# A transformer block on one core: when w2's first split is made, which banks attention takes, and a last product in full precision

## The chip, the core and the metric

The kernel runs on one core of a Trainium2 chip. The core has five engines with queues of their own: TensorE (PE, matrix products and transposes), VectorE (DVE), ScalarE (ACT), GpSimd (POOL) and SyncE (SP), which here only issues transfers. Each engine takes its instructions in program order, and an instruction that waits holds back all that stands behind it on the same engine. The metric is the device time of one execution in microseconds (us).

## What is computed

The reference adds to its input an attention over 16 heads and an MLP. Sizes: 2048 tokens of 448, 16 heads of 28 that share one key and one value, a hidden width of 1792, all in float32.

```python
xn = _layernorm(x)                                   # 2048 x 448
q = (xn @ wq).reshape(B, S, 16, 28).transpose(0, 2, 1, 3)
k, v = xn @ wk, xn @ wv                              # one head of 28
p = softmax(einsum("bhqd,bkd->bhqk", q, k) * 28 ** -0.5)
att = einsum("bhqk,bkd->bhqd", p, v) ... @ wo
mlp = gelu(_layernorm(xn) @ w1 + b1) @ w2 + b2       # gelu in its tanh form
out = x + att + mlp
```

The MLP normalises once more what is normalised already; the kernel folds both into one scale and shift per token (`lnq`, `lnqb`, beside `lnr`, `lnb` for the first alone).

## The kernel before

**Tiles.** The tokens lie in 16 tiles of 128. Four tiles make a chunk (`c`, 512 tokens, the width of a PSUM bank in float32). The core's eight PSUM banks are handed out by pools: `mp` has three, the others change from stage to stage. `mtile` takes the next bank of a ring of pools.

**Precision.** Most products run in the faster fp32r type with a value split into a high share and a low share: `wah`/`wal`, `w1h`/`w1l`, `w2h`/`w2l`, `hh`/`hl`, `oth`/`otl`, `woh`/`wol`, `xh`/`xl`. A split is one ACT copy (which rounds to the high share) and one subtraction on DVE or POOL. A product then takes three matmuls: high by high, high by low, low by high. Products of probabilities and values run in full float32, where the trace records each matmul twice.

**Stages.**

1. The front, about 0 to 66 us: for each chunk the statistics of the norm (`bn` L214 for one tile, `bn_end` from L216 for a chunk, with `rstd` L199 to L205), the centred rows (`center` L290 on ACT and L291 on POOL for columns 384 to 448), their transposes (`turn` L299 on PE, L300 on ACT, L301 on DVE) and four query slots (`q_slot`: PE L181 to L186, and an `evac` one slot later with DVE L390, ACT L391, DVE L398). Queries go to the DRAM tiles `qd` through the SBUF tiles `qe`, issued on the SP queue by L405. The first query slot also gives keys and values. Between the slots lie the splits of w1 (`w1_split`: ACT L355, POOL L356 and L357), in eight parts. Where each stands is written out by hand: in the tuple at L505, and in the table `more` filled at L438 to L459. The last argument of `later`, `ahead`, puts a job ahead of the slot's centring and turning.

2. The MLP, 66 to 463 us: 56 slots, one for each chunk and each of 14 blocks of 128 hidden columns. Slot n does `mlp1` of its own block (11 matmuls into one PSUM bank, `ph`; ACT L652 and L653 empty it; then POOL L654 and L655, ACT L658, POOL L659 and L660, ACT L665 for `hh`, POOL L667 for `hl`) and `mlp2` of the block of slot n - 2 (12 matmuls at L684, into four banks). The parts of the chain behind `mlp1` hang between the matmuls of `mlp2` by a table called `stages`. `ph` has one bank; slot 1 uses one of the four `m2` banks, which are not needed by then. w2's splits (`w2_split`: ACT L369, then `low`, L373 on DVE and on POOL, which also issues the next load of w2) stand in the slots of the first chunk. Between all those matmuls two further streams run: the row maxima for attention (`max_stream`: PE L570, DVE L571) and the turned scores (PE L604, DVE L605, ACT L622, stored to `td` by L625). Their pace is counted at L753 to L767.

3. Attention, 463 to 1068 us: 16 units of a chunk and four heads. Each step makes scores (PE L953), exponentials (ACT L954) and bursts of products of probabilities with values (PE L925) into a bank of the pool `op`. Seven banks in a ring serve the scores and the maxima. The row sums come out of the same products, and `norm_jobs` divides by them.

4. The end, for the last unit alone: `pv_halves` (L899) makes the last products in two halves of 256 tokens, one half in the `op` bank and one in the bank of `mp1`, which leaves the ring at that point. `end_jobs` (L865) divides each half by its row sums (DVE L879 to L882), splits it (ACT L883, DVE L884), multiplies with `woh` and `wol` (PE L815 to L817) and adds the sum to the rows (`rows`, from DRAM tile `ad`) by L819. The results leave by L821, on the ACT queue for odd tiles and on the SP queue for even ones. Matmuls of the identity (`spin`, L427) are put between the halves.

**What sets the order.** The program is emitted under a manual schedule, so on each engine the instructions run in the order in which Python emits them. Waits between engines follow from the tiles: who writes, who reads, and whose memory a tile takes over. The memory of `w2h` and `w2l` (pool `hp`, opened at L634) was before that of tiles of the front that were closed at L523.

Of the kernel before, what the change touches and what calls it, by code (L numbers as in the profile page):

```python
# [16 lines left out]
P = 128  # L17
S, D, H, DH, F = 2048, 448, 16, 28, 1792
NT = S // P
CT = 4  # L20
# [20 lines left out]
def block_kernel(ctx, tc, x, wq, wk, wv, wo, w1, b1, w2, b2, out):  # L41
# [322 lines left out]
    def w2_split(s):  # L364
        raw = wl_q.pop(0)
        ab = slice(2 * s, 2 * s + 2)

        def high():
            act.activation(w2h[:, ab, :], raw, AF.Copy)  # L369

        def low():
            for eng, b in ((dve, 0), (pool, 1)):
                eng.tensor_sub(w2l[:, 2 * s + b, :], raw[:, b], f(w2h[:, 2 * s + b, :]))  # L373
            if s + 2 < NF // 2:
                w2_load(s + 2)

        return high, low
# [103 lines left out]
    for c in range(NCH):  # L481
        if c + 1 < NCH:
            center, turn = norm_parts(c + 1, False, bank=lambda shape: (qbank, mtile)[next(turns) % 2](shape))
        for i in range(4):
# [20 lines left out]
            if i in ((2, 3), (1, 3), (1, 3), (0, 2))[c]:  # L505
                n = 2 * c + (i // 2 if c == 3 else i // 3)
                w1_split(n)
                if n < 2:
                    w1_load(n + 4)
                elif n == 3:  # L510
                    w1_load2(6)
                elif n in (4, 5):
                    w2_load(n - 4)
                if n == 2:
                    qms.append(load_m(*heads[0], q=pool))
                elif n in (4, 5):
                    load_m(TURNED[n - 4], 3, q3[n - 4], pool)
# [176 lines left out]
    def slot(n):  # L694
        nonlocal maxed, ending, later_low
# [30 lines left out]
    norms, maxed, ending, later_low = {}, 0, none, none  # L726
# [7 lines left out]
    for n in range(len(mslots) + 2):  # L734
# [73 lines left out]
    def o_jobs(c, gs, tiles=range(CT)):  # L808
        last = NG - 1 in gs
        for k in tiles:  # L810
# [9 lines left out]
            if last:  # L820
                (nc.scalar if k % 2 and c == NCH - 1 else nc.sync).dma_start(ov[:, CT * c + k, :], a)  # L821
# [43 lines left out]
    def end_jobs(u, pos, weighted):  # L865
# [3 lines left out]
        oth, otl = o_tiles(c, g)  # L869
        jobs = o_jobs(c, [g])  # L870
        tr, rb, on = att.tile([P, CW], F32, name="tr2", bufs=1), att.tile([P, CW], F32, name="tr", bufs=1), att.tile([P, CW], F32, name="oc", bufs=1)
# [5 lines left out]
        def shares(i):  # L877
# [4 lines left out]
            dve.tensor_mul(on[:, h], pos[i], rb[:, h])  # L882
            act.activation(oth[:, h], on[:, h], AF.Copy)  # L883
            return lambda: dve.tensor_sub(otl[:, h], on[:, h], f(oth[:, h]))  # L884
# [14 lines left out]
    def pv_halves(u, kt):  # L899
        nonlocal ring  # L900
# [135 lines left out]
```

## Time and profile before

| What | us |
|---|---|
| median of three runs | 1078.68 |
| those runs, lowest and highest | 1078.29, 1080.1 |
| the profiled execution's own time | 1079.98 |
| its span on the core | 1078.2 |

The granted TensorE clock of the profiled execution is 0.999. The span is what the profiler saw between the first and the last instruction on the core; the execution's own time has about 1.8 us more around it.

The profile's lines are read so. A line of the timeline has the start and the length in us, the engine, the line of the kernel, the operation, output <- input with the program's names, shape and type, and the number of instructions that follow each other; square brackets hold the idle time of the engine before it and what ended it. `PE` is a matmul, `SPq` or `ACTq` an instruction of an engine's queue that issues a transfer or handles a semaphore. A line of the windows has a stretch of the span, the busy time of PE, its weight loads, DVE, ACT and POOL with the number of instructions started, and then the granted clock, the mean busy share of the DMA engines and GB/s. A line of the waits has the engine and line, what it waited for, and total, times and longest. A group has the busy time, the mean in ns of one, and the idle time before them.

### The profile page before, as it was taken

The numbers are of one execution on the slowest core, as the hardware profiler recorded it, in microseconds if no ns is written. First come the engines' busy times: TensorE is split into PE (matmuls) and PEld (weight loads), VectorE is DVE, ScalarE is ACT, GpSimd is POOL, SyncE is SP. The second block draws the span as 40 slices with busy tenths as digits, with TensorE's granted clock in tenths as the row PEclk, the third lists the DMA queues.
The fourth block names the chain that finished last, engine by engine and source line by source line (L and its number), as shares of the span: only waits on it lengthen the run. The fifth ranks groups of instructions, "written<-read, shape, count | busy, mean of one in ns | idle before, by whom it ended". The sixth has DMA issues, their size and how long they took to land.

```text
span 1078.2 us, 17653 instructions
## 1 busy us (share of the span) xinstructions
PE 1068.5 (99%) x5869; PEld 720.0 (67%) x5869; DVE 906.7 (84%) x1825; ACT 721.8 (67%) x1254; POOL 574.8 (53%) x722
## 2 busy tenths in 40 slices
PE   9999999999999999999999999999999999999998
PEld 8778888888888888855555556555556555555455
DVE  6889999988988998977998997899896999876744
ACT  5675556666667666569677775677774777865784
POOL 5678897678777888744333532433352243243220
PEclk9999999999999999999999999999999999999999
DMA  8775546677877778687887798678896778985820
GB/s 268 242 214 150 143 126 175 167 190 189 211 179 195 181 209 220 157 181 165 184 200 186 173 218 193 160 188 195 194 205 174 180 168 189 213 191 141 187 43 35
DMA packets 139367, 193.54 MB, mean 179 GB/s; under 512 B 17078, under 2 KB 95084, under 8 KB 139276
## 3 DMA queue, kind: packets, MB, share of 16 engines
q1 hardware_dynamic: 126028, 169.59, 62.8%
q0 software_dynamic: 11840, 22.25, 9.1%
q8 instruction: 46, 0.75, 0.3%
q10 hardware_dynamic: 1408, 0.57, 0.2%
q14 instruction: 45, 0.37, 0.1%
HBM read 113.38 MB, written 77.71 MB: 177 GB/s over the span
## 4 chain that ended last, share of the span: by engine, by line
PE 96%; DVE 2%; ACT 1%; POOL 1%; issue 0%; POOLq 0%; ACTq 0%; DVEq 0%
PE po L925 21%; PE m L570 19%; PE m L953 17%; PE m L684 12%; PE ph L181 10%; PE m L604 5%; PE qp L181 2%; PE m L815 1%; PE m L816 1%; PE m L817 1%; PE ph L186 1%; PE ph L184 1%; PE m L427 1%; PE po L908 1%; PE m L908 1%
## 5 line engine op out<-in xcount | busy, mean ns | idle before, releaser
L571 DVE TENSOR_REDUCE mx<-m 128x1 f32<-128x512 f32 x784 | 507.3, 679 | 76.1 <-PE m L570 66.0
L954 ACT ACTIVATE p<-m 128x512 f32<-128x512 f32 x784 | 402.6, 609 | 160.8 <-PE m L953 160.6
L570 PE MATMUL m<-ks,qm 128*128 128x512 f32 x784 | 321.1, 410 | 0.7 <-DVE half L786 0.5
L953 PE MATMUL m<-xh,ks 128*128 128x512 f32 x784 | 257.4, 397 | 0.0
L925 PE MATMUL po<-p,vs 128*32 128x512 f32 x1920 | 230.9, 598 | 0.0
L570 PEld LDWEIGHTS m<-ks,qm 128*128 128x128 f32 x784 | 147.0, 187 | 114.9 <-ACT p L954 41.3
L605 DVE TENSOR_SCALAR_CACHE_REDUCE raw<-m 128x512 f32<-128x512 f32 x240 | 162.5, 690 | 17.5 <-PE m L604 10.6
L953 PEld LDWEIGHTS m<-xh,ks 128*128 128x128 f32 x784 | 146.1, 188 | 42.4 <-issue 6.2
L936 DVE STREAM_TRANSPOSE p<-half 128x1024 f32<-128x1024 f32 x120 | 148.3, 1236 | 5.3 <-PE m L908 2.0
L622 ACT ACTIVATE raw<-raw,m 128x1024 f32<-128x1024 f32 x120 | 133.1, 1150 | 0.8 <-DVE m L611 0.8
L925 PEld LDWEIGHTS po<-p,vs 128*32 128x32 f32 x1920 | 50.1, 109 | 114.0 <-issue 109.0
L652 ACT ACTIVATE hx<-ph,b1t 128x512 f32<-128x512 f32 x55 | 37.9, 690 | 129.9 <-PE ph L186 109.2
L604 PE MATMUL m<-ks,q 128*128 128x512 f32 x240 | 94.1, 392 | 0.1
L667 POOL TENSOR_TENSOR hl<-hx,hh 128x512 fp32r<-128x512 f32 x56 | 72.6, 1296 | 29.8 <-ACT hh L665 29.8
L684 PE MATMUL m<-w2l,hh 128*128 128x448 f32 x224 | 80.7, 365 | 1.3 <-DVE w2l L373 1.3
L684 PE MATMUL m<-w2h,hh 128*128 128x448 f32 x224 | 81.0, 364 | 0.0
L684 PE MATMUL m<-w2h,hl 128*128 128x448 f32 x224 | 80.8, 366 | 0.1
L557 POOL DMA_DIRECT2D xh<-mn x15 | 8.1, 539 | 133.5 <-ACT mn L553 133.5
L472 POOL DMA_DIRECT2D qm<-qd x120 | 61.6, 521 | 28.7 <-PE m L953 22.6
L655 POOL TENSOR_TENSOR hz<-hz,hx 128x512 f32<-128x512 f32 x56 | 72.7, 1298 | 4.7
L660 POOL TENSOR_TENSOR hx<-hx,hz 128x512 f32<-128x512 f32 x56 | 72.5, 1294 | 4.7
L535 POOL DMA_DIRECT2D xh<-qd x60 | 38.0, 634 | 51.4 <-PE m L570 49.1
(183 smaller groups left out, 1411.9 us busy)
## 6 DMA issues: line engine op xcount, KB each, us to landing
td<-raw SPq DMA_DIRECT2D x240, 256.0 KB
half<-td SPq DMA_DIRECT2D x120, 512.0 KB
xh<-qd POOLq DMA_DIRECT2D x60, 168.0 KB, 4.2
qm<-qd POOLq DMA_DIRECT2D x120, 56.0 KB, 4.3
qd<-qe SPq DMA_DIRECT2D x24, 256.0 KB
a<-in_A_x_dram SPq DMA_DIRECT2D x24, 224.0 KB
qm<-qd SPq DMA_DIRECT2D x76, 56.0 KB
ad<-a SPq DMA_DIRECT2D x16, 224.0 KB
```

The costliest lines, as they stand in the source:

```text
L181: pe.matmul(ps, w, v, start=(n == 0), stop=False)
L570: pe.matmul(pm, qm[:, t * P:(t + 1) * P], ks[:, n * CW:(n + 1) * CW], start=True, stop=True)
L571: dve.tensor_reduce(mx[:, CT * j + t, n:n + 1], pm, axis=AX.X, op=ALU.max)
L604: pe.matmul(sc, q3[i][:, t * P:(t + 1) * P], ks[:, n * CW:(n + 1) * CW], start=True, stop=True)
L605: dve.tensor_scalar(raw[:, :, 4 * n:4 * n + 4, :].rearrange("p r b i -> p b r i"), sc.rearrange("p (b r i) -> p b r i", r=4, i=32), SCALE, ...
L622: act.activation(raw[:, rs], raw[:, rs], AF.Exp, bias=m3[:, 4:5], scale=1.0)
L655: pool.tensor_mul(hz, hz, hx)
L684: pe.matmul(m2[k], h[:, k * P:(k + 1) * P], w[:, ft, :], start=(ft == 0 and i == 0), stop=(ft == NF - 1 and i == 2))
L925: pe.matmul(po[32 * j:32 * j + 32, :], vs[:, kt, :], ps.pop((u, kt, j)), start=(kt == 0), stop=(kt == NT - 1))
L936: dve.transpose(p.rearrange("p k (g j) -> p g k j", j=32), halves[u, kt // 8][:, :, 32 * (kt % 8):32 * (kt % 8) + 64].rearrange("p g (k j) ...
L953: pe.matmul(s, ks[:, kt * P:(kt + 1) * P], qss[u][:, j, :], start=True, stop=True)
L954: act.activation(p, s, AF.Exp, scale=SCALE)
```

## The change

It has five parts.

- Statistics of the front: three `bn` of chunk 2 stand at slot (0, 1) and one at (0, 2); those of chunk 3 stand at (1, 0), (1, 1), (1, 2) and (1, 3), the first of them not ahead of the slot's turning but behind it. Before, they stood one position later.
- w1's first split stands at slot (0, 1) in place of (0, 2); the load of w1's fifth part stays at (0, 2).
- w2's first split (`w2_split(0)`) is emitted whole at the start of slot 0, with both low halves on POOL. Before, its high half came in the stages of slot 0 and its low half in slot 2 behind `mlp1`, one half on DVE and one on POOL. The load of w2's third part, which `low` issues, moves with it.
- The last two slots of the MLP take their two row maxima early, and attention opens its pools in another order: `op` before `mp1`, and `mp1` fourth in the ring. At the end `mp1` leaves the ring seven steps before the last.
- In `end_jobs` the last product runs in full float32 on the divided values with `wor`; the splits, the spins and the twelve fp32r matmuls go. The row tile of k = 1 is added by a matmul with the identity and copied out by ACT; the other three are added by DVE.

```diff
@@ w2_split
         def low():
-            for eng, b in ((dve, 0), (pool, 1)):
+            for eng, b in ((pool if s == 0 else dve, 0), (pool, 1)):
                 eng.tensor_sub(w2l[:, 2 * s + b, :], raw[:, b], f(w2h[:, 2 * s + b, :]))
@@ front
-    for c, at in ((2, ((0, 1), (0, 2), (0, 2), (0, 3))), (3, ((1, 1), (1, 2), (1, 3), (2, 0)))):
+    for c, at in ((2, ((0, 1), (0, 1), (0, 1), (0, 2))), (3, ((1, 0), (1, 1), (1, 2), (1, 3)))):
         for k in range(CT):
-            later(*at[k], lambda t=CT * c + k: bn(t), c == 3)
+            later(*at[k], lambda t=CT * c + k: bn(t), c == 3 and k > 0)
...
-            if i in ((2, 3), (1, 3), (1, 3), (0, 2))[c]:
+            if (c, i) == (0, 2):
+                w1_load(4)
+            if i in ((1, 3), (1, 3), (1, 3), (0, 2))[c]:
                 n = 2 * c + (i // 2 if c == 3 else i // 3)
                 w1_split(n)
-                if n < 2:
-                    w1_load(n + 4)
+                if n == 1:
+                    w1_load(5)
@@ slot
             if n == 0:
-                high, later_low = w2_split(0)
+                for job in w2_split(0):
+                    job()
...
-        if n == 2:
-            later_low()
...
         if n == 0:
-            stages = {0: texp, 1: middle, 2: high}
+            stages = {0: texp, 1: middle}
@@ the loop over the slots
         if n >= len(mslots):
-            done, pace = 0, (2, 6)[ft]
+            done = 0
...
-            if n >= len(mslots) and done % pace == 1:
+            if n >= len(mslots) and (done % 2 if ft == 0 else done <= 2):
                 maxed += mxs.step()
@@ attention
     mp3 = ctx.enter_context(tc.tile_pool(name="mp3", bufs=3, space=PSUM))
+    op = ctx.enter_context(tc.tile_pool(name="op", bufs=1, space=PSUM))
     mp1 = ctx.enter_context(tc.tile_pool(name="mp1", bufs=1, space=PSUM))
-    op = ctx.enter_context(tc.tile_pool(name="op", bufs=1, space=PSUM))
-    ring = itertools.cycle([mp] * 3 + [mp3] * 3 + [mp1])
+    ring = itertools.cycle([mp] * 3 + [mp1] + [mp3] * 3)
@@ end_jobs
             dve.transpose(blocks(rb, h), rc[:, r, None].to_broadcast([P, 8, 32]))
-            dve.tensor_mul(on[:, h], pos[i], rb[:, h])
-            act.activation(oth[:, h], on[:, h], AF.Copy)
-            return lambda: dve.tensor_sub(otl[:, h], on[:, h], f(oth[:, h]))
+            for k in (0, P):
+                at = slice(256 * i + k, 256 * i + k + P)
+                dve.tensor_mul(on[:, at], pos[i][:, k:k + P], rb[:, at])
+
+        sums = {}
+
+        def product(k):
+            first = k not in sums
+            if first:
+                sums[k] = mtile([P, D])
+            pe.matmul(sums[k], on[:, k * P:(k + 1) * P], wor[:, g, :], start=first, stop=True)
+
+        def result(k):
+            a = rows[c, k]
+            if k == 1:
+                act.activation(a, sums[k], AF.Copy)
+            else:
+                dve.tensor_add(a, a, sums[k])
+            (nc.scalar if k % 2 else nc.sync).dma_start(ov[:, CT * c + k, :], a)
 
         weighted(0)
-        low = shares(0)
-        low()
+        shares(0)
         weighted(1)
-        spin(9, mtile([P, P]))
-        low = shares(1)
-        next(jobs)
-        low()
-        for _ in jobs:
-            pass
+        sums[1] = mtile([P, D])
+        pe.matmul(sums[1], ident, rows[c, 1], start=True, stop=False)
+        product(0)
+        product(1)
+        shares(1)
+        for k in (2, 3):
+            product(k)
+        for k in range(CT):
+            result(k)
@@ pv_halves and the loop over the steps
             pos[u] = [op.tile([P, CW], F32, name="po")[:, 0:256], mp1.tile([P, CW], F32, name="m")[:, 0:256]]
-            ring = itertools.cycle([b for b in (next(ring) for _ in range(7)) if b is not mp1])
...
+        if n == len(steps) - 7:
+            ring = itertools.cycle([b for b in (next(ring) for _ in range(7)) if b is not mp1])
```

More of the change, by code (lines that the diff above doesn't have):

```diff
@@ L694, in slot @@
     def slot(n):
-        nonlocal maxed, ending, later_low
+        nonlocal maxed, ending
         middle = high = low = none
@@ L724, in none @@
         pass
-    norms, maxed, ending, later_low = {}, 0, none, none
+    norms, maxed, ending = {}, 0, none
     mslots = [(c, ft) for c in range(NCH) for ft in range(NF)]
@@ L820, in o_jobs @@
             if last:
-                (nc.scalar if k % 2 and c == NCH - 1 else nc.sync).dma_start(ov[:, CT * c + k, :], a)
+                nc.sync.dma_start(ov[:, CT * c + k, :], a)
             yield
@@ L868, in end_jobs @@
         c, g = units[u]
-        oth, otl = o_tiles(c, g)
-        jobs = o_jobs(c, [g])
-        tr, rb, on = att.tile([P, CW], F32, name="tr2", bufs=1), att.tile([P, CW], F32, name="tr", bufs=1), att.tile([P, CW], F32, name="oc", bufs=1)
+        tr, rb, on = (att.tile([P, CW], F32, name=n, bufs=1) for n in ("tr2", "tr", "oc"))
         rc = att.tile([P, CW // 32], F32, name="rc", bufs=1)
@@ L881, in shares @@
             dve.transpose(blocks(rb, h), rc[:, r, None].to_broadcast([P, 8, 32]))
-            dve.tensor_mul(on[:, h], pos[i], rb[:, h])
-            act.activation(oth[:, h], on[:, h], AF.Copy)
-            return lambda: dve.tensor_sub(otl[:, h], on[:, h], f(oth[:, h]))
+            for k in (0, P):
[14 more added lines that the diff above has]
+            (nc.scalar if k % 2 else nc.sync).dma_start(ov[:, CT * c + k, :], a)
         weighted(0)
-        low = shares(0)
-        low()
+        shares(0)
         weighted(1)
-        spin(9, mtile([P, P]))
-        low = shares(1)
-        next(jobs)
-        low()
-        for _ in jobs:
-            pass
+        sums[1] = mtile([P, D])
[7 more added lines that the diff above has]
+            result(k)
     pos, ps, pairs = {}, {}, {}
     def pv_halves(u, kt):
-        nonlocal ring
         if kt == 0:
             pos[u] = [op.tile([P, CW], F32, name="po")[:, 0:256], mp1.tile([P, CW], F32, name="m")[:, 0:256]]
-            ring = itertools.cycle([b for b in (next(ring) for _ in range(7)) if b is not mp1])
         def weighted(i, kts):
```

## The prediction

> **What bounds the kernel now.** I read the page's busy shares first, then the chain of work that ended last, then TensorE's waits.
>
> ```profile
> PE 1068.5 (99%) x5869; PEld 720.0 (67%) x5869; DVE 906.7 (84%) x1825; ACT 721.8 (67%) x1254; POOL 574.8 (53%) x722
> PE 96%; DVE 2%; ACT 1%; POOL 1%; issue 0%; POOLq 0%; ACTq 0%; DVEq 0%
> ...
> PE m L684 <- DVE w2l L373: 1.3, 1, 1.3
> ...
> PE m L570 <- DVE half L786: 0.5, 1, 0.5
> PE m L815 <- ACT oth L883: 0.5, 1, 0.5
> ```
>
> TensorE is busy for 99% of the span and carries 96% of the last-ending chain. Its few waits happen once each, and the three quoted (waited in total, times, longest) are the ones that this diff touches. Only a wait removed or added, or TensorE work removed or added, moves the end: no PE gap behind a shift absorbs it, so a shift early in the span reaches the end at its full size. That makes the rest a matter of four places: front, start of the MLP, MLP to attention, and end.
>
> **Start of the MLP (w2's first split).** Before, the split's ACT half (L369) comes after slot 0's L652, L653 and L658, and its low halves (L373, one on DVE, one on POOL) only in slot 2. Afterwards L369 stands on ACT directly behind the last L391, ahead of L652 of slot 0, and both L373 stand on POOL ahead of L654. The wait that goes is the 1.29 us below. What the move exposes is the memory under w2h: it is that of the front's qe buffers, so L369 may write it only after the last of the front's stores from qe to qd (L405) has landed.
>
> ```profile
> 65.92 1.20 ACT L391 ACTIVATE qe<-qp 128x512 fp32r<-128x512 f32 x2 [0.57 <-ACT w1h L355]
> 68.47 0.69 ACT L652 ACTIVATE hx<-ph,b1t 128x512 f32<-128x512 f32 x1 [1.35 <-PE ph L186]
> 69.05 0.68 ACT L653 ACTIVATE hz<-ph,b1s 128x512 f32<-128x512 f32 x1
> 71.94 0.63 ACT L658 ACTIVATE hz<-hz 128x512 f32<-128x512 f32 x1 [0.27 <-POOL hz L655]
> 72.47 0.94 ACT L369 ACTIVATE w2h<-raw 128x896 fp32r<-128x896 f32 x1
> 74.69 0.63 ACT L665 ACTIVATE hh<-hx 128x512 fp32r<-128x512 f32 x1
> ...
> 64.61 4.70 SPq L405 DMA_DIRECT2D qd<-qe  x8
> ...
> 71.50:72.00 0.50, 0.50 (x4) 0.42 (x3) 0.50 (x2) 0.23 (x2) 0.41 (x1) 1.00 0.01 4
> 72.00:72.25 0.25, 0.25 (x3) 0.21 (x2) 0.25 (x1) 0.25 (x1) 0.00 (x0) 1.00 0.00 0
> ...
> L369 ACTq EVENT_SEMAPHORE  x4: 38/38/161, 71.9 to 72.3; - x4
> ...
> 69.89 0.63 POOL L654 TENSOR_SCALAR hz<-hz 128x512 f32<-128x512 f32 x1 [2.07 <-ACT hz L653]
> 76.62 1.28 POOL L667 TENSOR_TENSOR hl<-hx,hh 128x512 fp32r<-128x512 f32 x1
> ...
> L373 POOL TENSOR_TENSOR w2l<-raw,w2h 128x448 fp32r<-128x448 f32 x7 | 8.1, 1162 | 0.0
> ...
> 72.30 0.39 PE L181 MATMUL ph<-xh,w1h 128*128 128x512 f32 x1
> 75.70 0.36 PE L684 MATMUL m<-w2h,hh 128*128 128x448 f32 x1
> 78.43 0.66 PE L684 MATMUL m<-w2l,hh 128*128 128x448 f32 x2 [1.29 <-DVE w2l L373]
> 79.79 0.77 PE L684 MATMUL m<-w2h,hl 128*128 128x448 f32 x3
> 80.84 0.39 PE L181 MATMUL ph<-xh,w1h 128*128 128x512 f32 x1
> ```
>
> The SP queue issues the eight stores back to back until 64.61 + 4.70 = 69.31 us. The DMA share (second column from the end) falls to 0.01 only in 71.5 to 72.0 and to nothing in 72.0 to 72.25. ACT's sequencer still spent 161 ns, against 38 for the others, on one of the four waits put in front of L369, between 71.9 and 72.3. So the stores land at about 72.2, and before, L369 at 72.47 simply came late enough. Ahead of L652 it has no such cover: ACT is free at 65.92 + 1.20 = 67.12 and would stand until 72.5. Queued behind it on ACT are L652 and L653 of slot 0 (who empty the one ph bank), then that slot's turned exponentials and L658; on POOL L654 and L655.
>
> Step by step:
> - L369 runs 72.50 to 73.35 (next start 0.85 later, as 72.47 to L652 in the old order), L652 to 73.93, L653 to 74.61. TensorE's next use of ph, slot 2's mlp1, starts at 74.66 in place of 72.30: **+2.36**. Its block lasts 75.70 - 72.30 = 3.40 and ends at 78.06.
> - POOL makes both low halves from 73.5 (2 x 1.16 and a little between: 75.88), then L654. From L654's start to L665's end took 74.69 + 0.63 - 69.89 = 5.43 before, all of it one chain (L654, L655, L658, L659, L660, L665), so hh is there at 81.31. The first product with w2h starts at 81.35 instead of 75.70: **+5.65**, with a second gap of 81.35 - 78.06 = 3.3 us.
> - From there the products do not wait for w2l: 80.84 - 75.70 = 5.14 less 1.45 (the 1.29 and what the restart adds at its edges) gives 3.69, to 85.04. hl comes from L660's end (80.6), L654 and L655 for slot 1 (0.63, and about 1.3 as for L667, a tile of the same size) and L667 (1.28): 83.9; the products that need it are due at 81.35 + (79.79 - 75.70 - 1.45) = 83.99. In time.
> - The next mlp1 needs ph emptied by ACT, whose L652 waits for L667 to give hx back (83.9), then 0.58 + 0.68: 85.2. Against 80.84 this is **+4.3** net, the 1.45 gain included.
>
> Bounds: the stores could have landed at 72.0, which gives 3.9; at 72.3 and with 0.1 more at each of the handovers 4.6. The added SP step, the load of the next w2 pair, waits in its queue for L373 and has only the first td stores behind it, which only attention reads.
>
> **Front.** w1's first split (ACT 0.94, POOL's two) moves ahead of an L391 at 20 us; three bn_stats of chunk 2 move together into (0,1); chunk 3's start one position earlier, one of them before L390 instead of after it.
>
> ```profile
> 28.73 1.02 DVE L199 TENSOR_SCALAR rs<-lnp 128x4 f32<-128x4 f32 x2
> 42.25 0.62 DVE L214 BATCH_NORM_STATS2 st<-hl 128x6 f32<-128x448 f32 x1
> 43.18 0.55 DVE L199 TENSOR_SCALAR rs<-lnp 128x4 f32<-128x4 f32 x2
> ...
> 28.01 1.64 POOL L356 TENSOR_TENSOR w1l<-raw,w1h 128x672 fp32r<-128x672 f32 x1
> 42.00 1.63 POOL L356 TENSOR_TENSOR w1l<-pair,w1h 128x672 fp32r<-128x672 f32 x1 [0.76 <-ACT w1h L355]
> ```
>
> Taking the bn at 42.25 out looks like a gain, but L199 does not end by its own length: the first pair ends at 29.75, 0.10 after POOL's L356 ends (29.65), the second at 43.73, 0.10 after 43.63. So at 43 us nothing comes earlier, as long as POOL's L356 stays where it is. At 28 us L356 itself comes some tenths earlier, since the first split no longer stands ahead of it on POOL and ACT, but the chunk-3 bn ahead of L390 (0.62) takes that back before TensorE sees it. I take **0.0**. Low end -1.2, if L199 got in ahead of L356 at both places and a bn of 0.62 were saved at each; high end +0.6, one bn on the path. The Trainium skill, "GPSIMD Engine Reference", 1. Specifications, has GpSimd's SBUF access shared with VectorE, with contention for some DVE instructions. By that rule L199 stays held and the front gives 0; without it the front would give up to 1.2, and the two equal ends above bear the rule out.
>
> **MLP to attention.** The last slot's row maxima are spread differently: the second of them now falls into the wait for hl. Attention's PSUM ring takes op before mp1 and hands out mp1 fourth, so the fourth bank no longer waits for L689's last add; the fifth does.
>
> ```profile
> 461.42 0.68 PE L684 MATMUL m<-w2h,hl 128*128 128x448 f32 x2
> 463.40 0.40 PE L953 MATMUL m<-xh,ks 128*128 128x512 f32 x1
> 463.61 1.14 DVE L689 TENSOR_TENSOR a<-a,m 128x448 f32<-128x448 f32 x2
> 464.80 0.50 PE L570 MATMUL m<-ks,qm 128*128 128x512 f32 x1 [0.54 <-DVE half L786]
> ...
> 465.57 3.05 ACT L954 ACTIVATE p<-m 128x512 f32<-128x512 f32 x6 [0.59 <-PE m L953]
> ```
>
> The products with hl wait a moment for L667 ahead of 461.42; a maximum fills that. Matmuls of 512 columns start 0.23 apart (15 of them in the 3.40 from 72.30 to 75.70), so the first score comes 0.23 earlier. Then the fourth matmul no longer waits to 464.80; the next one waits for L689's end, 464.75 less about 0.4 (0.23 from the products, the rest because no maximum stands between the adds any more): 464.35. ACT's third exponential follows at 464.8 instead of 465.57. ACT paces the next steps, so I take **-0.75**; bounds -0.3 (the shift at the first score alone, with the bank wait back one matmul later) and -1.0. Once the ring turns, it is the same seven banks.
>
> **End.** Nine spins and twelve fp32r products (woh, wol, otl) give way to one identity product that adds the row tile, and four products in full fp32; L883 and L884 go.
>
> ```profile
> 1070.01 0.42 DVE L884 TENSOR_TENSOR otl<-oc,oth 128x256 fp32r<-128x256 f32 x1 [0.48 <-ACT oth L883]
> 1070.35 0.44 DVE L879 STREAM_TRANSPOSE tr<-m 128x256 f32<-128x256 f32 x1
> 1071.54 0.42 DVE L882 TENSOR_TENSOR oc<-m,tr 128x256 f32<-128x256 f32 x1
> 1072.79 1.88 DVE L819 TENSOR_TENSOR a<-a,m 128x448 f32<-128x448 f32 x3
> ...
> 1068.48 2.27 PE L427 MATMUL m<-ident 128*128 128x128 f32 x18
> ```
>
> No fp32 product of 448 columns is in the trace. The spins are fp32, each on record twice: 18 records of 128 columns in 2.27, the last of which shows its whole pipeline; at some 0.111 a record, 448/128 = 3.5 and two records give 0.78. From below, an L684 product's 0.20 spacing (fp32r, same columns) times three is 0.6; from above 2.27/18 x 3.5 x 2 = 0.88. I take 0.78.
> The second transpose no longer has the L884 and its 0.48 wait in front, only the second half of a multiply: it starts at about 1069.52, 0.83 earlier, so the second half's first multiply starts near 1070.75 and the block's third product at 1071.1 (the identity product and the first two products lie before it, from 1068.5 to 1070.95). Two products of 0.78 end at 1072.66, 0.17 more to be seen: DVE's last add runs 1072.87 to 1073.48. Before, the last of the three ended at 1072.79 + 1.88 = 1074.67. The stores behind stay the same: **-1.2**; by the bounds of the product -0.8 to -1.5.
>
> **The sum.** +4.3 + 0.0 - 0.75 - 1.2 = +2.35. The profiled execution took 1079.98 us (1078.2 of span and 1.8 around it); with the change 1082.3. It lay 1.30 above the median 1078.68, so beside the runs shown the forecast is 1081.0. Its own range is 1079.9 (3.9 - 0.2 - 1.0 - 1.5 = 1.2) to 1082.2 (4.6 + 0.3 - 0.5 - 0.9 = 3.5).
>
> **Rivals.**
> B, the clock drops in the second PE gap. For it: TensorE starts slow, as these rows of the spins show:
>
> ```profile
> 4.00:8.00 4.00, 4.00 (x23) 4.00 (x22) 3.17 (x13) 2.60 (x5) 2.25 (x4) 1.00 1.04 329
> 8.00:12.00 4.00, 4.00 (x38) 4.00 (x37) 3.08 (x15) 2.67 (x6) 2.31 (x7) 1.00 0.94 267
> ```
>
> 23 matmuls in 4 us, then 38. A gap of 3.3 us with one of 2.4 before it could bring that back. Against it: after the 1.29 us wait at 78.43 the products keep their 0.2. No row has a longer gap. At half speed for some 4 to 5 us, about half of that is lost: +2.2, 1083.2. The Trainium skill, "TensorE: Matmul & The Clock Gate", Part 1, puts the return to the slow clock after about 3.4 us without work and its practical table warns of gaps over some 3 us; by that rule the gap here is at the edge, and the time would be 1083.2.
> C, the front's chain runs free: 1081.0 - 1.2 = 1079.8. Against it the two ends at POOL's L356 above.
> D, the other side: L369 doesn't wait, because the stores have landed before slot 0's ph is full (by about 68.5). Then the stall goes (-1.45), with -0.75 and -1.2 it makes -3.4: 1075.3. It decides at ACT's L369: a start before 68.5. Against it stands the DMA share until 71.5; for it, that the 161 ns may be another semaphore's.
> E, the end gains nothing, since fp32 products take two to four times the estimate or the reordered tail waits elsewhere: 1081.0 + 1.2 to 1.9, some 1082.6.
>
> **Chances.** Forecast 0.56, B 0.20, C 0.06, D 0.12, E 0.06. Two in ten are left out by 1078.2 to 1084.2, which takes in C, B and E and leaves out D with some over. 0.2% is 2.16 us (about what a measurement tells from no change), so slower begins at 1080.84 and faster at 1076.5: slower holds B, E and a little over half of the forecast (0.32), 0.58; faster is D, 0.12; within 0.30.
>
> **What would show it.** ACT's L369 waiting from 67.1 to about 72.5, a PE gap near 70 to 74.7 and one near 78 to 81.3, no gap at the first w2l product, and the slot-3 mlp1 4.3 later; L199 still ending with POOL's L356; the third L954 of attention 0.75 earlier relative to the slots before it; products in full fp32 about 0.78 apart. If L369 starts before 70 the forecast is wrong at its main term; if the matmuls between 81 and 86 are spaced twice as far, B holds.

## The result and the profile after

| | median us | runs | lowest to highest |
|---|---|---|---|
| before | 1078.99 | 8 | 1078.26 to 1080.12 |
| changed | 1082.39 | 8 | 1081.65 to 1083.66 |

The ratio is 1.0032, with a 95% interval of 1.0021 to 1.0043: the change costs 2.3 to 4.6 us, 3.4 by the medians. The profiled execution took 1081.89 us, with a span of 1080.0.

The first view is TensorE's waits of the changed kernel (total, times, longest). Line numbers have moved: from L508 to L700 they are two higher than before, further down by another amount (L786 is L787, L908 is L923, L953 is L968).

```profile
PE m L686 <- ACT hh L667: 2.9, 1, 2.9
PE ph L181 <- ACT hz L655: 1.5, 1, 1.5
...
PE m L968 <- DVE half L787: 0.2, 1, 0.2
```

The wait for w2l is gone, and two waits that weren't there head the list. Next, the timelines of SP, ACT, POOL and TensorE at the start of the MLP:

```profile
62.52 5.42 SPq L405 DMA_DIRECT2D qd<-qe  x8
...
65.18 1.20 ACT L391 ACTIVATE qe<-qp 128x512 fp32r<-128x512 f32 x2 [0.57 <-ACT w1h L355]
70.99 0.95 ACT L369 ACTIVATE w2h<-raw 128x896 fp32r<-128x896 f32 x1 [4.62 <-DVE mx L573]
71.85 0.67 ACT L654 ACTIVATE hx<-ph,b1t 128x512 f32<-128x512 f32 x1
72.42 0.68 ACT L655 ACTIVATE hz<-ph,b1s 128x512 f32<-128x512 f32 x1
...
79.10 0.63 ACT L667 ACTIVATE hh<-hx 128x512 fp32r<-128x512 f32 x1 [0.93 <-POOL hx L662]
...
72.02 2.24 POOL L373 TENSOR_TENSOR w2l<-raw,w2h 128x448 fp32r<-128x448 f32 x2 [4.95 <-ACT w2h L369]
74.35 0.63 POOL L656 TENSOR_SCALAR hz<-hz 128x512 f32<-128x512 f32 x1
...
73.15 0.50 PE L181 MATMUL ph<-xh,w1h 128*128 128x512 f32 x1 [1.47 <-ACT hz L655]
...
76.46 0.39 PE L186 MATMUL ph<-xl,w1h 128*128 128x512 f32 x1
79.79 0.74 PE L686 MATMUL m<-w2h,hh 128*128 128x448 f32 x1 [2.94 <-ACT hh L667]
...
83.96 0.77 PE L686 MATMUL m<-w2h,hl 128*128 128x448 f32 x3
...
85.00 0.40 PE L181 MATMUL ph<-xh,w1h 128*128 128x512 f32 x1
```

ACT stands for 4.62 us between its last L391 and L369, 3.05 us past the end of the last issue of a store to qd (62.52 + 5.42 = 67.94). The view puts that wait down to a maximum on DVE (L573); L369 reads and writes nothing that a maximum does, so the event that came last by the profile is not the one that held it. ACT's queue tells more. It handles five waits ahead of L369 (min, median and max in ns):

```profile
L369 ACTq EVENT_SEMAPHORE  x5: 38/38/4840, 65.8 to 70.9; - x5
```

The first of them took 4.84 us. In the trace it stands on the semaphores of the first and the last store to qd. The last store's got its last update at 70.61; the queue went on at 70.64, and the four short waits behind it brought L369 to 70.99. Behind L369 come L654 and L655, then TensorE's slot 2, then POOL's chain, then the first products: the two gaps of the forecast. The second gap has a sequel, in the windows of the changed kernel (last columns: granted clock, DMA share, GB/s):

```profile
79.70:83.00 3.30, 3.21 (x8) 2.81 (x9) 1.38 (x2) 2.42 (x5) 3.18 (x4) 0.51 0.26 59
83.00:86.00 3.00, 3.00 (x15) 2.57 (x15) 2.33 (x4) 3.00 (x4) 2.92 (x3) 0.98 0.97 234
```

For 3.3 us behind the gap the granted clock is 0.51, and TensorE starts 8 matmuls where it later starts 15 in 3.0 us.

To see where the time went over the whole span, the start of the same matmul (the n-th of its kind) was compared between the profiled executions. The table has its start less that in the kernel before, in us; the columns beside the changed kernel's are experiments of the next section.

| at (us, before) | changed | w2_only | front_only | tail_only | end_only | low_mid | own_mem |
|---|---|---|---|---|---|---|---|
| 9.5 | -0.54 | -0.57 | -0.59 | -0.67 | -0.56 | -0.54 | -0.67 |
| 72 | -0.78 | -0.62 | -0.74 | -0.70 | -0.64 | -0.47 | -0.45 |
| 90 | +3.84 | +4.25 | -0.68 | -0.71 | -1.95 | -1.89 | -1.22 |
| 459 | +3.91 | +4.34 | -0.76 | -0.64 | -1.94 | -1.90 | -1.02 |
| 465 | +3.16 | +4.31 | -0.77 | -1.39 | -1.96 | -2.60 | -1.76 |
| 480 | +3.50 | +4.31 | -0.75 | -1.04 | -1.95 | -2.27 | -1.41 |
| 1036 | +3.83 | +4.33 | -0.80 | -0.68 | -1.86 | -2.07 | -1.20 |
| 1038 | +3.04 | +4.33 | -0.80 | -1.47 | -2.65 | -2.86 | -1.98 |
| end of span | +1.8 | +4.2 | -0.9 | -1.5 | -3.8 | -4.2 | -3.3 |

The first row belongs to no change: every one of these executions is about 0.6 ahead at 9.5 us, so the profiled execution of before was late there. The spins show why: they start 0.21 us apart and then 0.11, in before from 7.4 us on and in the changed kernel from 4.7 us on. So between 4 and 8 us TensorE starts 33 matmuls in the changed kernel and 23 in before:

```profile
4.00:8.00 4.00, 4.00 (x33) 3.83 (x32) 3.19 (x13) 2.56 (x5) 2.24 (x4) 1.00 1.06 348
```

The clock's column can't show it, here or in the forecast's rows, since the record of the clock begins only at 4.64 us in this execution and at 7.38 in that of before. The execution of spin_both, an experiment of the next section whose spins quicken at 7.3 us, is 0.06 ahead at 9.5 us.

From then on the changed kernel gains 0.24 in the front (a wait of 0.43 at 27.9 us, for xl from DVE, is gone), loses 4.62 at the start of the MLP, gains 0.75 at 465 us and gives nearly all of it back by 1036, gains 0.79 at one place at 1037 us, and 1.24 at the end. Without the first row that is +2.3; the medians have +3.4.

The 1037 us step is a wait of TensorE that the kernel before has and the changed one has not; their TensorE timelines:

```profile
1036.14 0.64 PE L908 MATMUL po<-p,vs 128*32 128x256 f32 x8
1037.36 0.64 PE L908 MATMUL m<-p,vs 128*32 128x256 f32 x8 [0.58 <-ACT p L954]
```

```profile
1039.97 0.64 PE L923 MATMUL po<-p,vs 128*32 128x256 f32 x8
1040.43 0.61 PE L923 MATMUL m<-p,vs 128*32 128x256 f32 x8
```

There the last unit's second half takes the bank of mp1. Before, by the releaser named, a score in that bank was still being read by ACT's exponential.

The end in the changed kernel, DVE and then TensorE:

```profile
1072.14 0.49 DVE L883 TENSOR_TENSOR oc<-po,tr 128x128 f32<-128x128 f32 x2
1072.55 0.44 DVE L878 STREAM_TRANSPOSE tr<-m 128x256 f32<-128x256 f32 x1
...
1073.74 0.49 DVE L883 TENSOR_TENSOR oc<-m,tr 128x128 f32<-128x128 f32 x2
...
1075.15 1.37 DVE L898 TENSOR_TENSOR a<-a,m 128x448 f32<-128x448 f32 x2 [0.39 <-PE m L891]
...
1072.49 3.37 PE L891 MATMUL m<-wor,oc 128*128 128x448 f32 x8
```

Four products (eight records) take 3.37 with two short waits in them. The last add ends at 1076.52, which is 1.85 after the one of before (1074.67), and TensorE's last burst ahead of the end was 3.05 late: 1.20 gained.

### The profile page after: what moved, and what is told of

It is laid out like the page before. It is cut to its first block, busy times and chain, and to the rows that moved or that the text cites. A ratio compares the mean times of both kernels' runs of the same rounds, so it can differ in the third digit from the quotient of the medians.

```text
span 1080.0 us, 17607 instructions
## 1 busy us (share of the span) xinstructions
PE 1068.7 (99%) x5849; PEld 717.9 (66%) x5849; DVE 903.6 (84%) x1823; ACT 721.3 (67%) x1253; POOL 574.7 (53%) x723
## 4 chain that ended last, share of the span: by engine, by line
PE 94%; DVE 3%; DMA 1%; ACT 1%; POOL 1%; issue 0%; SPq 0%; ACTq 0%; DVEq 0%
PE po L940 21%; PE m L572 19%; PE m L968 17%; PE m L686 13%; PE ph L181 10%; PE m L606 5%; PE m L817 1%; PE m L816 1%; PE m L818 1%; PE ph L184 1%; PE ph L186 1%; PE qp L181 1%; DMA qd<-qe 1%; PE po L923 1%; PE m L923 1%; DVE qe L398 0%
## 5 line engine op out<-in xcount | busy, mean ns | idle before, releaser
L573 DVE TENSOR_REDUCE mx<-m 128x1 f32<-128x512 f32 x784 | 507.5, 680 | 81.2 <-PE m L572 71.1
L968 PE MATMUL m<-xh,ks 128*128 128x512 f32 x784 | 257.9, 398 | 0.2 <-DVE half L787 0.2
L607 DVE TENSOR_SCALAR_CACHE_REDUCE raw<-m 128x512 f32<-128x512 f32 x240 | 162.3, 690 | 20.0 <-PE m L606 10.7
L968 PEld LDWEIGHTS m<-xh,ks 128*128 128x128 f32 x784 | 146.2, 188 | 43.5 <-ACT p L969 6.0
L654 ACT ACTIVATE hx<-ph,b1t 128x512 f32<-128x512 f32 x55 | 37.9, 689 | 129.2 <-PE ph L186 111.6
L669 POOL TENSOR_TENSOR hl<-hx,hh 128x512 fp32r<-128x512 f32 x56 | 72.4, 1293 | 30.2 <-ACT hh L667 30.1
L662 POOL TENSOR_TENSOR hx<-hx,hz 128x512 f32<-128x512 f32 x56 | 72.2, 1290 | 4.7
L181 PE MATMUL ph<-xh,w1h 128*128 128x512 f32 x165 | 65.1, 395 | 1.5 <-ACT hz L655 1.5
```

What stands on the lines that cost most here:

```text
L181: pe.matmul(ps, w, v, start=(n == 0), stop=False)
L573: dve.tensor_reduce(mx[:, CT * j + t, n:n + 1], pm, axis=AX.X, op=ALU.max)
L607: dve.tensor_scalar(raw[:, :, 4 * n:4 * n + 4, :].rearrange("p r b i -> p b r i"), sc.rearrange("p (b r i) -> p b r i", r=4, i=32), SCALE, ...
L968: pe.matmul(s, ks[:, kt * P:(kt + 1) * P], qss[u][:, j, :], start=True, stop=True)
```

## The experiments

Each kernel was timed beside the kernel before on the same chip:

| run | what | median us | before, same chip | ratio (95%) |
|---|---|---|---|---|
| undo_w2 | changed, w2's split back | 1077.59 | 1079.46 | 0.9985 (0.9976 to 0.9994) |
| w2_only | before, only w2's split moved | 1083.90 | 1079.46 | 1.0043 (1.0030 to 1.0057) |
| end_only | before, only the end | 1077.61 | 1079.46 | 0.9986 (0.9977 to 0.9994) |
| tail_only | before, only pace and banks | 1078.72 | 1079.46 | 0.9995 (0.9986 to 1.0004) |
| front_only | before, only the front | 1078.84 | 1079.44 | 0.9998 (0.9990 to 1.0007) |
| spin_fill | changed, second gap filled | 1082.19 | 1079.44 | 1.0033 (1.0021 to 1.0045) |
| spin_both | changed, both gaps filled | 1082.12 | 1078.57 | 1.0033 (1.0020 to 1.0045) |
| stores_split | changed, stores on two queues | 1082.76 | 1079.44 | 1.0038 (1.0025 to 1.0050) |
| own_mem | undo_w2, early copy elsewhere | 1076.68 | 1078.57 | 0.9982 (0.9973 to 0.9991) |
| low_mid | undo_w2, DVE's half sooner | 1076.45 | 1079.44 | 0.9977 (0.9968 to 0.9987) |
| old_banks | low_mid, old order of banks | 1076.07 | 1079.66 | 0.9969 (0.9959 to 0.9980) |
| old_pace | low_mid, old pace of maxima | 1076.68 | 1079.66 | 0.9974 (0.9965 to 0.9984) |

### One part of the change at a time

w2's part is the hunk of the diff on `w2_split` and the one on `slot`, of which the main lines stand here; undo_w2 takes the part back out of the changed kernel, w2_only puts it alone into the one before.

```diff
             if n == 0:
-                high, later_low = w2_split(0)
+                for job in w2_split(0):
+                    job()
...
-            stages = {0: texp, 1: middle, 2: high}
+            stages = {0: texp, 1: middle}
```

> The changed kernel with w2's first split put back (L369 behind slot 0's tanh, the low halves in slot 2 on DVE and POOL). Theory, the wait for the stores to qd costs the time: without it only the front (0 to -0.2), the start of attention (-0.5 to -0.75) and the end (-1.2) are left, 1.7 to 2.2 us under the kernel before, and TensorE's two gaps near 72 and 78 are gone while the 1.3 us wait for DVE's w2l is back. Rival, the split's place is not what costs, and the loss lies in the ring of banks or the end: slower than before by 3 us or more.

> The kernel before with only w2's first split moved. Theory: 4.3 to 5.5 us slower than before (3.9 to 4.6 by the forecast's sum, up to 1.5 more where TensorE runs slow behind the second gap, less what the gap gives back at 78.4 and 87.7 us). Rival, the loss needs the front's moved statistics and w1 split too: under 2 us slower.

By the medians undo_w2 lies 1.9 us under before (0.6 to 2.6 by the interval), w2_only 4.4 over it (3.2 to 6.2). The loss is w2's split, and it needs nothing else of the change. Only the times of undo_w2 are used here; that the gaps go with the old place of L369 is read further down from low_mid, where L369 stands as in undo_w2 and TensorE has no wait on record between 46 and 462 us.

For the end, the front and the passage into attention the same parts of the diff were put into the kernel before one by one.

> The kernel before with only the end in full float32. Theory: the span from the first of DVE's last transposes to the last add is 1.2 us shorter (0.8 to 1.5), and the time 0.8 to 1.5 us under that of before. Rival, the identity product and the four long products only move the wait: within 0.3 us of before.

> The kernel before with only the row maxima of the MLP's last two slots and the order of attention's banks changed. Theory: 0.4 to 0.8 us under before, seen as scores that start earlier at 465 us and keep that. Rival, ACT's exponentials pace the first steps, so the gain is lost again before the first burst of products with the values: within 0.2 us of before.

> The kernel before with only the front's changes, the statistics and w1's first split. Theory, VectorE's L199 is held to the end of POOL's L356 and the moved work gains nothing: within 0.3 us of before. Rival, the chain from the statistics to the centred rows gets shorter: 0.6 to 1.2 us under before.

The span of end_only's end is 1.2 shorter, as the theory had it (-2.64 at 1067 us, -3.8 at the end of the span). Its time is 1.85 under before by the medians and 0.6 to 2.6 by the interval, which can't tell 1.2 from more. The trace can: the line that takes mp1 out of the ring seven steps earlier belongs to this part and brings the 0.79 at 1037 us besides (-1.86 to -2.65). Its profile also has -0.64 to -1.95 at the start of the MLP, where it is the same program as before; that is the next heading's matter. tail_only shows that the 0.75 at 465 us is mostly lost by 1036 (-1.39 to -0.68, with -0.64 at 459), as the rival had it, if not for its reason alone: half of that goes between 480 and 1036 (-1.04 to -0.68), past the first steps. What is left of tail_only's gain is the step at 1037, which it has too. front_only is level with before by its interval (1.1 under to 0.8 over), as the theory said; its trace gains 0.15.

### The old wait for w2l is not always there

end_only has the kernel before's program up to attention, but the wait that the forecast wanted to win back is 0.2 us there, not 1.3. Its wait and its timelines of DVE and POOL, then DVE's in the kernel before:

```profile
PE m L684 <- DVE w2l L373: 0.2, 1, 0.2
...
76.01 0.63 DVE L373 TENSOR_TENSOR w2l<-raw,w2h 128x448 fp32r<-128x448 f32 x1 [0.31 <-ACT raw L622]
...
76.03 1.75 POOL L667 TENSOR_TENSOR hl<-hx,hh 128x512 fp32r<-128x512 f32 x1
```

```profile
76.65 1.72 DVE L373 TENSOR_TENSOR w2l<-raw,w2h 128x448 fp32r<-128x448 f32 x1 [0.31 <-POOL hz L655]
```

In end_only DVE's L373 starts 0.02 ahead of POOL's L667 and takes 0.63, and L667 takes 1.75. In the kernel before L667 starts at 76.62, 0.03 ahead of L373, takes its usual 1.28, and L373 takes 1.72. In these two executions the one that starts first runs at its own speed and the other stands. The Trainium skill, "SBUF — State Buffer", section SBUF: two separate sides, says just that of a VectorE operation with two SBUF inputs and a GpSimd operation: the first holds their shared port for its whole length. The trace agrees, with 0.63 against 1.72. In front_only the two start 0.01 us apart, DVE first by the record, and yet it is L373 that takes 1.76; so close together the record doesn't tell the order. A few hundredths of a us decide about a wait of 1.3 us. Four profiled executions have the old split as before: in before, front_only and tail_only TensorE waits 1.3 us for w2l, in end_only 0.2.

### What holds L369

> The changed kernel with half of chunk 3's stores to qd issued on POOL's queue instead of SP's. Theory, ACT's L369 stands until the last of these stores has landed: SP's issues end about 2 us earlier, L369 starts 1 to 2 us earlier, and the time falls by about as much (more, if the gap gets too short for the slow clock). Rival, L369 waits for something else, the load of w2 or the maxima on DVE: L369 starts within 0.3 us of where it was, and the time is the same or higher by the issues on POOL.

```diff
                 for j in range(2):
-                    nc.sync.dma_start(qd[j][rows, cols], f(qe[at, j, :]))
+                    q = nc.gpsimd if c == NCH - 1 and j else nc.sync
+                    q.dma_start(qd[j][rows, cols], f(qe[at, j, :]))
```

This one missed its aim. stores_split's timeline of POOL, then of ACT:

```profile
65.49 1.66 POOL L356 TENSOR_TENSOR w1l<-pair,w1h 128x672 fp32r<-128x672 f32 x1
67.23 0.66 POOL L357 TENSOR_TENSOR w1h<-pair,w1h 64x224 fp32r<-64x224 f32 x1
67.84 1.10 POOL L406 DMA_DIRECT2D qd<-qe  x2
...
71.81 0.95 ACT L369 ACTIVATE w2h<-raw 128x896 fp32r<-128x896 f32 x1 [5.33 <-PE m L186]
```

POOL's last two stores stand behind L356 and L357 and are issued until 68.94, later than SP's 67.94 in the changed kernel. L369 moved with them, by 0.82. From the end of the last issue to L369 it is 3.05 in the changed kernel and 2.87 here. That fits the stores, and here too the trace names them: ACT's queue stands on the semaphore of POOL's second store, which landed at 71.35, and goes on at 71.38. The next run takes the cause away.

> The changed kernel with w2's first split put back where it was, and one more early copy of the split's first block at the place that the change chose (ACT behind the last L391, POOL ahead of L654), in tiles of their own that no store to qd reads; slot 2's products of chunk 0 use that copy. Theory, it is the memory of the qe tiles that holds L369: the early copy starts near 66 us without a wait, TensorE's gaps near 72 and 78 stay away, the old 1.3 us wait for w2l goes too, and the time is 2.5 to 3.6 us under before, 1.0 to 1.5 us under the kernel with the split only put back. Rival, the early split itself costs ACT and POOL their time ahead of slot 0, wherever it writes: a gap ahead of slot 2's mlp1 remains, and the time is no better than with the split put back.

```diff
+    own = [hrp.tile([P, CW], F32R, name=n)[:, 0:D] for n in ("hh", "hl")]
...
+        if s == 0:
+            act.activation(own[0], raw[:, 0], AF.Copy)
+            pool.tensor_sub(own[1], raw[:, 0], f(own[0]))
...
+            w = own[w is w2l] if (c, ft) == (0, 0) else w[:, ft, :]
```

The copy at the same place in ACT's queue, written to other memory, in own_mem's ACT timeline:

```profile
65.50 1.20 ACT L395 ACTIVATE qe<-qp 128x512 fp32r<-128x512 f32 x2 [0.57 <-ACT w1h L356]
66.59 0.57 ACT L369 ACTIVATE hh<-raw 128x448 fp32r<-128x448 f32 x1
68.07 0.69 ACT L658 ACTIVATE hx<-ph,b1t 128x512 f32<-128x512 f32 x1 [0.90 <-PE ph L187]
```

It reads the same w2 rows and starts at once, at 66.59, and slot 0's first instruction waits for TensorE alone. No gap follows (-0.45 at 72 us, -1.22 at 90). So it is neither the load of w2 nor ACT's time, but the memory that the split writes; and by the semaphores above it is the stores out of that memory that have to land. By the ratios, 0.9982 against 0.9985, own_mem and undo_w2 can't be told apart, so the theory's second number, 1.0 to 1.5 us under undo_w2, was not borne out. One reason stands in own_mem's waits: in place of the old wait for w2l a new one of 0.8 us, on maxima that queue behind DVE's L373 (L377 here), which is still made for the later chunks.

```profile
PE m L576 <- DVE mx L577: 0.8, 1, 0.8
```

### The clock behind the gaps

> The changed kernel with 12 identity matmuls more, ahead of the first products with w2h, where TensorE stands still for 2.9 us. They take 12 x 0.23 = 2.7 us and fit in that gap. Theory, the products behind the gap start at half speed because TensorE stood still: with the gap filled they are 0.2 us apart from the first on, the block from the first product with w2h to the next block's first matmul takes 3.7 instead of 5.2 us, and the time falls by about 1.2 to 1.5 us, less what hl then makes wait. Rival, those products are slow because of something else (weights late, PSUM): no change, or slower by a few tenths.

> The changed kernel with identity matmuls in both gaps, 7 (1.6 us) ahead of slot 2's mlp1 and 12 (2.7 us) ahead of its first products. With the second gap alone filled, the slow stretch was seen behind the first gap instead. Theory, TensorE's speed falls behind such a gap, whichever of the two: with both filled no stretch of matmuls between 71 and 85 us is spaced at half speed, and the time is 1.2 to 1.6 us under the changed kernel, some 1.8 to 2.2 us over before. Rival, the slow stretch comes whatever TensorE did before it: about 3.3 us over before, as the changed kernel.

```diff
+            if n == 2:
+                spin(7, mtile([P, P]))
             middle, ending = yield from mlp1(*mslots[n])
...
+        if n == 2:
+            spin(12, mtile([P, P]))
```

spin_fill has only the second of these. Windows of spin_fill, then of spin_both:

```profile
73.30:77.40 4.10, 3.96 (x10) 3.15 (x11) 1.40 (x4) 1.86 (x4) 3.18 (x5) 0.59 0.37 112
77.40:81.00 3.60, 3.60 (x28) 3.34 (x27) 1.55 (x5) 2.64 (x4) 3.43 (x4) 1.00 0.00 0
```

```profile
71.00:80.30 9.30, 9.12 (x59) 8.01 (x57) 4.70 (x12) 5.53 (x9) 6.64 (x7) 1.00 0.15 49
80.30:84.20 3.90, 3.81 (x17) 3.04 (x17) 2.77 (x5) 2.98 (x6) 3.77 (x4) 1.00 0.38 82
```

In spin_fill's execution the clock had dropped already behind the first gap (a wait of 1.78 us), where the changed kernel's execution kept its speed behind one of 1.47. The length of the wait alone doesn't decide: stores_split keeps its speed behind a first wait of 2.18 us and slows only behind its second. The next windows are 3.41 us long, which is the length of every slow stretch on record; two are of spin_fill, cut where its clock changes, and two of stores_split:

```profile
70.60:74.01 3.41, 1.63 (x7) 1.04 (x6) 1.56 (x3) 2.72 (x4) 1.70 (x2) 1.00 0.00 0
74.01:77.42 3.41, 3.41 (x9) 2.67 (x8) 1.40 (x4) 1.17 (x3) 2.49 (x4) 0.50 0.45 135
```

```profile
70.20:73.62 3.42, 1.59 (x8) 0.97 (x6) 2.09 (x4) 1.81 (x3) 0.78 (x1) 1.00 0.06 23
73.62:77.03 3.41, 3.06 (x13) 2.55 (x14) 1.84 (x5) 1.33 (x2) 3.23 (x4) 1.00 0.21 39
```

A slow stretch lasts 3.41 us at a clock of 0.50 in each of the four executions that have one (changed, w2_only, spin_fill, stores_split). In the window of 3.41 us ahead of it TensorE was busy for 0.16 to 0.19 of the time in three of them and for 0.48 in spin_fill (1.63 of 3.41). In stores_split it was busy for 0.46 (1.59 of 3.42) and the clock held. Where the limit lies is open.

With both gaps filled there is no slow stretch: spin_both's first products start at 80.39 and the next mlp1 at 84.25, 3.86 us later, against 85.00 - 79.79 = 5.21 in the changed kernel. So the slow stretch comes from the gaps, and makes that block 1.35 longer where it falls behind the second. The rival, that the products would be slow anyhow, is out. But the time hardly moved (1.0033 both, against 1.0032), and no gain in time is shown. In the traces TensorE falls back by 4.62 between 72 and 90 us in the changed kernel and by 3.78 in spin_both, so 0.84 of the 1.35 is left there. Of that, spin_both loses 0.6 near 434.8 us, at a wait that the changed kernel lacks, for a tile of the turned scores:

```profile
PE m L606 <- DVE raw L607: 0.4, 1, 0.4
```

That wait is not the spins' doing: old_banks, which has none, has it too (0.7). It is there in some executions and not in others.

### Versions that beat both

> The changed kernel with w2's high half as before the change and DVE's low half in the middle of slot 2's mlp1, POOL's low half behind it as before. Theory: the old wait for w2l (1.3 us, 1.45 with its restart) shrinks or goes since that half is ready before 78.4 us, so the time is 2.5 to 3.6 us under before, 0.8 to 1.4 us under the changed kernel with w2's split only put back. Rival, the half on VectorE waits for L369 and for POOL in its new place too and holds back L605, whose banks TensorE needs: no gain over that kernel.

```diff
+            g = mlp1(*mslots[n])
+            if n == 2:
+                g = with_job(g, 5, lambda: later_low(((dve, 0),), False))
+            middle, ending = yield from g
         if n == 2:
-            later_low()
+            later_low(((pool, 1),))
```

`with_job` calls its job behind the fifth matmul. The half then runs between two L607, ahead of POOL's subtraction for hl (L669 here, at 76.53), and TensorE takes the w2l products without a wait; low_mid's DVE and TensorE:

```profile
74.00 0.71 DVE L373 TENSOR_TENSOR w2l<-raw,w2h 128x448 fp32r<-128x448 f32 x1
...
76.50 0.56 PE L686 MATMUL m<-w2l,hh 128*128 128x448 f32 x2
```

1076.45 is 3.0 us under before by the medians (1.4 to 3.5 by the interval), and the theory's range was 2.5 to 3.6. The advantage over undo_w2 (0.9977 against 0.9985) lies within the intervals.

> The version with DVE's low half in slot 2's mlp1 (1076.45), with attention's pools and ring in the order of the kernel before, and everything else as there. Theory, the early maxima of the last two slots earn about 1 us ahead of 464 us, and it is the new order of banks that gives most of it back between 480 and 750 us: TensorE stays about 1 us ahead to the end, and the time is 0.3 to 0.6 us lower. Rival, ACT's pace gives it back whatever the banks: the same time within 0.2 us, or higher, where the fourth bank again waits for the last of L689's adds.

> The same version with the row maxima of the last two slots at their old places and the new order of banks kept. Theory, the pace earns the 1 us before 464 us, the banks the rest of what is seen at 466 us: TensorE is level with the kernel before at 463 us, and the time is 0 to 0.4 us higher than with the new pace, since most of that gain is given back anyway. Rival, pace and banks only help together: the time is 0.5 us or more higher.

From 459 us to 1036 us old_banks goes from -0.76 to -1.15, low_mid from -1.90 to -2.07, old_pace from -1.94 to -1.76: the early maxima earn and keep 0.4 with the old banks, and the new order of banks gives back 0.2 of it. (Between 90 and 459 us old_banks' execution lost 0.95 and low_mid's nothing, though the two have the same program there; 0.8 of that lies at the wait for a turned score named above.) The times (0.9969, 0.9977, 0.9974) can't tell these apart. All three beat before and after.

## Why the prediction held, and where it didn't

The time, 1082.39, lies in the range of 1078.2 to 1084.2 and in the direction given; the likeliest value, 1081.0, was 1.4 low. It lies 0.2 above the forecast's own range (1079.9 to 1082.2), which was narrower than its terms allow: it took -0.2 and +0.3 for the front, -0.5 for attention and -0.9 for the end, where the text gave -1.2 and +0.6, -0.3 and -0.8. By the forecast's steps:

- **L369 waits for the stores.** Right, and shown by own_mem and the semaphores. The start was given as 72.5, from a landing at 72.2; the landing was at 70.61 and the start at 70.99. Of the 1.5, 0.78 is that the whole execution ran ahead there; the rest goes with the last issue of a store, which ended 1.37 sooner (67.94 against 69.31), 0.6 more than that shift.
- **First gap, +2.36.** Was 73.15 - (72.30 - 0.78) = 1.63, smaller by what L369 came sooner.
- **Second gap, +5.65 at the first product.** Was 4.09 + 0.78 = 4.87. From L656's start (74.35) to the end of L667 (79.10 + 0.63) it took 5.38, against the 5.43 that the forecast copied from before.
- **The products behind it, 3.69.** This step failed: they took 5.21, as rival B had it, at a granted clock of 0.51. B came together with the forecast rather than in its place, and at 1.35 to 1.5 in place of 2.2, since the slow stretch lasted 3.4 us and not 4 to 5. The Trainium skill, "TensorE: Matmul & The Clock Gate", Part 1, has the clock watch a free-running window of about 3.4 us; the slow stretches of 3.41 us fit that length, but its table's return to the slow clock after a whole idle window does not fit the drop in spin_fill, where TensorE was busy for 1.63 of the 3.41 us ahead of it.
- **Sum for w2, +4.3.** Was 4.62 (changed) and 4.87 (w2_only), against a profiled execution of before that had the long w2l wait. That the term came out near was luck: a chain 0.8 too long and a clock taken as steady (1.5) have opposite signs, and 0.3 is won back at 87.7 us, which the forecast didn't have.
- **The 1.45 won back.** This term was mis-sized: it was read from one execution in which L373 lost the race with L667. In end_only the same wait is 0.2. In an execution of before without the wait the move has nothing to win there. That could be a part of why the medians differ by 3.4 where the two profiles differ by 2.3, but it isn't shown: how often the wait is there was not counted, and the changed kernel, which has no such wait, spreads as widely from run to run as the one before (1081.65 to 1083.66).
- **Front, 0.0.** Was -0.24 in the changed kernel and -0.15 in front_only; the time level. The wait at 27.9 us is gone, so the chunk-3 statistics do not take all of that gain back, as the forecast had it. L199 is held as forecast. It starts at 41.93 in place of 43.18 and still ends 0.10 behind POOL's L356. From the changed kernel's DVE and POOL:

```profile
41.93 1.07 DVE L199 TENSOR_SCALAR rs<-lnp 128x4 f32<-128x4 f32 x2
...
41.28 1.62 POOL L356 TENSOR_TENSOR w1l<-pair,w1h 128x672 fp32r<-128x672 f32 x1 [0.57 <-ACT w1h L355]
```

- **MLP to attention, -0.75.** Was 3.91 - 3.16 = 0.75 at 465 us, and 0.08 at 1036. The step that failed is "once the ring turns, it is the same seven banks": a seven-bank cycle in another order is not the same cycle. With the old order old_banks keeps its place from 480 us on (-1.11 to -1.15); with the new one low_mid, old_pace, tail_only and the changed kernel lose 0.1 to 0.4 from there to 1036.
- **A term that was missing.** The line "PE m L908 <- ACT p L954", 0.6 us, stood in the list of waits of before, between the ones that were quoted as those the diff touches. Both the new order of banks and the earlier leaving of mp1 remove it: 0.79.
- **End, -1.2.** Was -1.17 to -1.24. A product in full float32 takes 0.75 where its records follow without a wait; the estimate from the spins was 0.78.
- **Rival D** is excluded by L369's 4.62 us of standing, C by L199's ends, E by the end's 1.2.

## What to carry to other kernels

Before an instruction is moved forward, look at who used the memory that it writes: its old place may be late enough to hide a wait that the profile shows nowhere. When a wait is to be won back, ask in how many executions it is there; one between two engines that start within 0.03 us of each other is there in some only. A gap on TensorE can cost more than its length: here the matmuls behind it ran at half speed and one block took 1.35 longer. The whole list of waits should be held against a change of banks, not only the waits that it was made for.

## What the runs showed of the hardware that was not expected

- Behind waits of 2.94 us and of 1.78 us the granted clock fell to 0.50 for 3.41 us. Behind one of 1.47 and one of 2.18, in other executions, it didn't.
- The spins at the start of the program quicken from 0.21 to 0.11 us apart at a time that differs from execution to execution, from 4.7 us (changed) to 7.4 us (before).
- A subtraction on DVE of 128x448 took 0.63 or 1.72, and POOL's subtraction of 128x512 1.28 or 1.75, by which of the two started first (0.02 to 0.03 us apart).
